# A fused attention and two-layer-pair MLP on one core: gathered score blocks in four fixed tiles, cleared once

## The chip, the core and the metric

The kernel runs on one core of a Trainium2 chip. The time is the device time of one execution in microseconds (us); before the change three runs gave a median of 1237.27 us. TensorE (PE) multiplies matrices, VectorE (DVE) and ScalarE (ACT) work elementwise and empty PE's accumulators, GpSimd (Pool) does small elementwise work, and SyncE (SP) issues every DMA. Each engine takes its instructions in the order in which the program lists them.

## What is computed

```python
scores = scale * np.matmul(q, k.transpose(0, 1, 3, 2))          # 4 batches, 12 heads, 448 rows, 64 wide
scores = np.einsum('bhij,hg->bgij', scores, w_pre)              # heads mixed
attn = softmax(scores)                                          # max, exp, sum + 1e-9, divide
attn = np.einsum('bhij,hg->bgij', attn, w_post)                 # heads mixed again
x = np.matmul(attn, v)                                          # -> (1792, 768)
h = x @ w_in;  y = (h * np.clip(h + 3, 0, 6) / 6) @ w_out       # 768 -> 2048 -> 768
out = (((y @ w1) * (y @ w2)) @ w3) @ w4                         # 768 -> 1024 -> 1024 -> 768
```

## The kernel before

The program is written by a planner. Every step (`plan.add`) has an engine or a choice of engines, a cost, a priority and the steps that it needs; `Plan.run` plays the steps through with these costs and writes each engine's instructions in the order that comes out. `URGE` is the table of offsets that sets the priorities, so a change of one number can move steps on every engine.

Attention runs in 92 blocks, 23 to a batch. A chunk of 100 to 120 query rows is scored (`sc`: PE, six steps per chunk, each emptied by ACT or DVE into a tile `s`). From batch 1 on, q and k are split first into a high and a low half by Pool (`qhl`, `khl`, a cast and a subtraction for each piece). Then each block goes through these steps:

1. `blank` (L461): Pool clears the upper 4 rows of a tile `g`, of which there are four. Rows 4 to 123 come from the next step; the clearing is needed since the matmuls read from row 0.
2. `gather` (L471): SP issues two DMAs that collect the 12 heads of ten query rows each out of `s` into `g`.
3. `premix` (PE, `pre`): four matmuls on `g` mix the heads.
4. `rowmax` (DVE, `m`), two `softexp` (ACT, `e`, with the sums in `z`).
5. `guard` (L496, Pool, or DVE when Pool is planned to be busy for longer than `pGuard`): adds 1e-9 to `z`; `recip` (DVE, `r`), `weigh` (DVE, `wt`).
6. `postmix` (PE, `post`): 32 small matmuls, emptied in two copies by ACT or DVE into `pth` or `ptl`.

After 11 or 12 blocks `values` (PE, `val`) multiplies by v. Scores, premix, postmix and values share four accumulator tiles `pp`. The MLPs follow (`up`, `dn`, `w`), and their first `up` steps are interleaved with the last blocks. They reuse the tiles of attention: `t`, `v` and `gs` lie in the tiles of `g` or `e`.

Of the kernel before, what the change touches and what calls it, by code (L numbers as in the profile page):

```python
# [11 lines left out]
F32 = mybir.dt.float32  # L12
F32R = mybir.dt.float32r
# [7 lines left out]
B, H, S, D = 4, 12, 448, 64  # L21
# [11 lines left out]
BEFORE = 64 - ROWS  # L33
# [16 lines left out]
def query_order():  # L50
# [9 lines left out]

URGE = dict(pPool=13.287, pACT=19737.186, pDVE=67509.792, pOut=0.285, pGuard=376.043, pCopy=1.57, pRest=75.72, pEvac=56.516, load0=33.466, load=-4.77, gather=-168.494, pre=-140.104, max=-8.516, exp=27.495, norm=15.87, post=2.04, evac=43.38, values=32.185, step=8.267, vload=-54.801, vload0=-30.207, lead=-15.369, begin=-9.6, consts=-75.04, moe=102.08, rows=-66.313, win=-123.444, wout=-22.784, w34=60.769, w2=92.263, unit0=3.845, unit1=6.661, down1=78.626, unit2=12.371, down2=55.186, wo=-0.083, wd=-56.448, narrow=-92.743, sums=98.663, w34us=69.836, pHalf=621.884, halve=10.141)


SHARED = dict(
    accs=("pth",), kraw=("q",), qraw=("q",), khl=("k",), qhl=("u",), act0=("s",), act3=("s",), t=("g", "e"), v=("g", "e"), gs=("g", "e"), graw=("k",),
    w=("k", "u", "w"), block=("w", "u", "k"), raw=("q", "raw", "e"), early=("w0", "w1", "w2", "k", "u"), first=("q", "r0", "r1", "r2", "raw"), stg=("x",), stage=("raw", "w"),
    wo=tuple(f"z{i}" for i in range(9)) + ("w0", "w1", "w2") + tuple(f"y{i}" for i in range(28)),
    wd=tuple(f"z{i}" for i in range(6, 9)) + ("w0", "w1", "w2") + tuple(f"v{i}" for i in range(28)),  # L70
# [160 lines left out]
def attention_moe(ctx: ExitStack, tc, qd, kd, vd, consts, w_in, w_out, w1, w2, w3t, w4, out):  # L231
    nc = tc.nc
# [25 lines left out]
    def pool(name, side=left, **kw):  # L258
# [11 lines left out]
    BUFS = {  # L270
        "s": (kp, [120, H, S], F32, 2), "k": (kp, [128, 2, S], F32, 6), "q": (kp, [128, 2, S], F32, 3), "u": (kp, [128, DM], F32, 4),
        "kraw": (kp, [128, 2, S], F32, 0), "qraw": (kp, [128, DM], F32, 0), "khl": (kp, [128, 2, S], F32R, 0), "qhl": (kp, [128, DM], F32R, 0),
        "e": (kp, [128, 2, S], F32, 4), "g": (kp, [128, 2, S], F32, 4), "gs": (kp, [128, 2, S], F32R, 0), "t": (kp, [128, 2, S], F32, 0),
        "act0": (kp, [128, 2, KC, S], F32R, 0), "act3": (kp, [128, 2, KC, S], F32R, 0), "o": (None, [128, 2, S], F32, 2),
        "v": (kp, [128, 2, S], F32, 0), "graw": (kp, [128, 2, S], F32, 0),
        "w": (None, [128, DM], F32R, 1), "raw": (None, [128, DM], I32, 3), "block": (None, [128, 2, DM // 2], F32R, 0),
# [21 lines left out]
    def take(*bufs):  # L298
        for x in bufs:
            shape, dtype = BUFS[x.kind][1:3]  # L300
            p, part, _, n = BUFS[x.tag]
            if p == "x":
                x.t = late["acts"][part // 4].rearrange("p a (h c) s -> p (a h) c s", h=2)[:, part % 4]
            elif p == "y":
                x.t = late["acts"][part // 7].rearrange("p a c s -> p (a c s)")[:, part % 7 * DM:(part % 7 + 1) * DM]
            elif p == "z":
                x.t = late["z"][part // 3][:, part % 3]
            elif p == "acts":
                x.t = late["acts"][part]
            elif isinstance(part, int):  # L310
                x.t = late[p][:, part]
            else:
                p = late[p or "pool"] if isinstance(p, (str, type(None))) else p
                x.t = p.tile(shape, dtype, tag=x.tag, name=x.kind, bufs=max(n, 1))
# [26 lines left out]
    direct, gathers, loads = [], {}, []  # L341
# [8 lines left out]
    def constants():  # L350
        raw = Buf("consts")
        dma_in(URGE["consts"], consts, raw, ns=300)

        def emit():
            x = raw.t
            own, own2 = x[:, 2 * H:2 * H + SET], x[:, 2 * H + SET:]
            nc.vector.memset(wih[:, ROWS:], 0.0)
            nc.vector.scalar_tensor_tensor(
                out=wih[:, :ROWS].rearrange("p (i g) -> p i g", i=SET), in0=x[:, :H].unsqueeze(1).to_broadcast([128, SET, H]),
                scalar=D ** -0.5, in1=own.unsqueeze(2).to_broadcast([128, SET, H]), op0=ALU.mult, op1=ALU.mult)  # L360
            nc.vector.tensor_tensor(
                out=wip, in0=x[:, H:2 * H].unsqueeze(2).to_broadcast([128, H, SET]),
                in1=own2.unsqueeze(1).to_broadcast([128, H, SET]), op=ALU.mult)
        plan.add("DVE", 700, -6, emit, use=(raw,))
# [88 lines left out]
    def mix(s):  # L453
# [4 lines left out]
        both = range(min(2, G0[4] - 2 * t))  # L458
        used = slice(0, PIECE * len(both))

        def blank():  # L461
            take(g)
            nc.gpsimd.memset(g.t[:BEFORE], 0.0)  # L463
        blanked = plan.add("Pool", 900, at + URGE["gather"] - 1, blank, new=(g,))
        for y in both:
            G = 2 * t + y
            c = next(c for c in range(4) if G < G0[c + 1])
            p0, d = G - G0[c], GROUPS[c]
            st = stile[4 * b + c]

            def gather(y=y, st=st, p0=p0, d=d):  # L471
                nc.sync.dma_start(out=g.t[BEFORE:BEFORE + 2 * ROWS, y], in_=st.t[p0:p0 + 9 * d + 1:d])  # L472
            gathers[s, y] = plan.add("SP", 1250, at + URGE["gather"], gather, read=(st,), after=(blanked,), hold=(g,), chain=("g", s), issue=760)
            g.writers.append(gathers[s, y])

        def premix():
# [68 lines left out]
    def values(prio, u, hq):  # L545
# [38 lines left out]
        for pr in range(2):  # L584
            stored.setdefault((u // 2, 2 * hq + pr), []).append(op)

    constants()
    for ci in range(16):
        s0 = cstart[ci - 1] * U0 + URGE["begin"] if ci else -120
# [573 lines left out]
```

## Time and profile before

| | us |
|---|---|
| three runs | 1231.84, 1237.27, 1242.02 |
| profiled execution, its own time | 1233.19 |
| its span, first to last instruction | 1231.4 |
| PE busy in it | 1201.4 |
| DVE, ACT, Pool busy in it | 798.5, 521.5, 220.2 |

The profiled execution took 1233.19 us by the clock of the runs, 1.8 us more than its span. A matmul counts as busy from its start to its modelled end, and matmuls overlap, so the idle time of PE is a surer figure than its busy time. "Issue" as a releaser stands for an idle time at whose end the profile sees no event.

### The profile page before, as it was taken

The numbers are of one execution on the slowest core, as the hardware profiler recorded it, in microseconds if no ns is written. First come the engines' busy times: TensorE is split into PE (matmuls) and PEld (weight loads), VectorE is DVE, ScalarE is ACT, GpSimd is POOL, SyncE is SP. The second block draws the span as 40 slices with busy tenths as digits, with TensorE's granted clock in tenths as the row PEclk, the third lists the DMA queues.
The fourth block names the chain that finished last, engine by engine and source line by source line (L and its number), as shares of the span: only waits on it lengthen the run. The fifth ranks groups of instructions, "written<-read, shape, count | busy, mean of one in ns | idle before, by whom it ended". The sixth has DMA issues, their size and how long they took to land.

```text
span 1231.4 us, 29262 instructions
## 1 busy us (share of the span) xinstructions
PE 1201.4 (98%) x12048; PEld 999.6 (81%) x12048; DVE 798.5 (65%) x1348; ACT 521.5 (42%) x1003; POOL 220.2 (18%) x428
## 2 busy tenths in 40 slices
PE   8899999999989999999999999999999999999998
PEld 3566656666668899999999999998889988999997
DVE  3787677767788789414777777417777688853210
ACT  7767566566664443212333333213433332332110
POOL 2476664844244200001000000000000000000000
PEclk9999999999999999999999999999999999999999
DMA  6654755736768777724899898716843222433311
GB/s 224 198 164 166 231 171 159 231 130 197 224 178 272 226 262 263 257 73 160 265 302 291 280 334 297 266 47 226 305 140 111 93 82 82 144 122 137 105 60 46
DMA packets 105357, 231.53 MB, mean 188 GB/s; under 512 B 10152, under 2 KB 53512, under 8 KB 105224
## 3 DMA queue, kind: packets, MB, share of 16 engines
q1 hardware_dynamic: 105224, 229.66, 56.6%
q8 instruction: 95, 1.56, 0.5%
q14 instruction: 38, 0.31, 0.1%
HBM read 132.31 MB, written 58.61 MB: 155 GB/s over the span
## 4 chain that ended last, share of the span: by engine, by line
PE 83%; DMA 4%; issue 3%; ACT 3%; POOL 2%; DVE 2%; SPq 2%; POOLq 0%; ACTq 0%; DVEq 0%
PE up L239 34%; PE dn L239 29%; PE w L239 5%; PE post L239 5%; PE sc L239 4%; PE pre L239 4%; PE val L239 3%; DMA qraw<-qd 1%; SPq L472 1%; DMA stg<-xdram 1%; ACT e L492 1%; POOL g L463 1%; ACT ptl L334 0%; DMA stage<-xdram 0%; ACT pth L334 0%
## 5 line engine op out<-in xcount | busy, mean ns | idle before, releaser
L239 PE MATMUL dn<-gs,act 128*128 128x448 f32 x1080 | 222.9, 366 | 0.0
L239 PEld LDWEIGHTS dn<-gs,act 128*128 128x128 f32 x1080 | 202.8, 188 | 17.5
L239 PE MATMUL up<-act,block 128*128 128x448 f32 x1008 | 206.8, 366 | 2.4 <-ACT t L1065 0.9
L239 PE MATMUL up<-act,w 128*128 128x448 f32 x1008 | 205.1, 365 | 0.0
L239 PEld LDWEIGHTS up<-act,block 128*128 128x128 f32 x1008 | 188.7, 188 | 20.1 <-ACT t L1065 2.1
L239 PEld LDWEIGHTS up<-act,w 128*128 128x128 f32 x1008 | 189.3, 188 | 14.5
L695 ACT ACTIVATE raw<-raw 128x384 f32<-128x384 f32 (+1 forms) x140 | 73.6, 528 | 172.4 <-DMA raw<-w 51.1
L239 PEld LDWEIGHTS post<-wt,e 60*64 60x64 f32 x5760 | 99.8, 135 | 55.3 <-issue 24.9
L492 ACT ACTIVATE e<-pre,m 128x448 f32<-128x448 f32 (+1 forms) x184 | 116.4, 635 | 35.6 <-DVE m L486 17.5
L486 DVE TENSOR_REDUCE m<-pre 128x2 f32<-128x896 f32 (+1 forms) x92 | 99.9, 1086 | 39.8 <-PE pre L239 39.5
L242 DVE TENSOR_TENSOR gs<-graw,gs 128x896 fp32r<-128x896 f32 x48 | 52.1, 1088 | 104.0 <-ACT gs L334 101.3
L239 PE MATMUL post<-wt,e 60*64 60x60 f32 x5760 | 107.1, 220 | 9.9 <-issue 4.2
L239 PE MATMUL dn<-gs,wo 128*128 128x448 f32 x456 | 101.6, 368 | 0.0
L463 POOL MEMSET g<- 4x896 f32 x92 | 76.6, 835 | 108.5 <-PE pre L239 95.2
L239 PE MATMUL pre<-g,wih 64*64 64x448 f32 x720 | 93.2, 560 | 2.6 <-issue 1.7
L239 PEld LDWEIGHTS dn<-gs,wo 128*128 128x128 f32 x456 | 85.6, 188 | 8.0
L242 POOL TENSOR_TENSOR early<-raw,wo 128x768 fp32r<-128x768 f32 x1 | 1.8, 1848 | 458.9 <-ACT wo L334 458.9
L334 ACT CAST gs<-graw 128x896 fp32r<-128x896 f32 x44 | 41.3, 939 | 91.4 <-PE dn L239 77.7
L710 DVE SCALAR_TENSOR_TENSOR raw<-raw 128x384 int32<-128x384 int32 (+1 forms) x140 | 71.7, 544 | 0.0
L708 DVE SCALAR_TENSOR_TENSOR raw<-raw 128x384 int32<-128x384 int32 (+1 forms) x140 | 70.6, 541 | 1.6
L817 DVE SCALAR_TENSOR_TENSOR t<-t,up 128x896 f32<-128x896 f32 x32 | 34.7, 1084 | 56.6 <-ACT t L814 56.1
L242 DVE TENSOR_TENSOR block<-raw,block 128x384 fp32r<-128x384 f32 x112 | 60.6, 560 | 14.7 <-ACT block L334 14.0
(87 smaller groups left out, 1496.7 us busy)
## 6 DMA issues: line engine op xcount, KB each, us to landing
g<-s SPq DMA_DIRECT2D x180, 210.0 KB
raw<-w SPq DMA_DIRECT2D x48, 384.0 KB
g1dram<-t SPq DMA_DIRECT2D x32, 448.0 KB
graw<-g1dram SPq DMA_DIRECT2D x32, 448.0 KB
raw<-w_out SPq DMA_DIRECT2D x32, 384.0 KB
raw<-w_in SPq DMA_DIRECT2D x28, 384.0 KB
raw<-w3t SPq DMA_DIRECT2D x32, 256.0 KB
g2dram<-t SPq DMA_DIRECT2D x32, 224.0 KB
```

The source lines that it names most:

```text
L239: nc.tensor.matmul(o, lhsT=lt, rhs=rh, start=start, stop=stop, **kw)
L242: eng.tensor_tensor(out=o, in0=a, in1=b, op=ALU.subtract)
L334: nc.scalar.copy(o, i)
L463: nc.gpsimd.memset(g.t[:BEFORE], 0.0)
L472: nc.sync.dma_start(out=g.t[BEFORE:BEFORE + 2 * ROWS, y], in_=st.t[p0:p0 + 9 * d + 1:d])
L486: nc.vector.tensor_reduce(out=m.t[used], in_=pre.t[used, :, :S], axis=AX.X, op=ALU.max, negate=True)
L492: nc.scalar.activation(out=e.t[used, a_], in_=pre.t[used, a_, :S], func=ACTF.Exp, bias=m.t[used, a_:a_ + 1], accum_out=z.t[used, a_:a_ + 1])
L695: nc.scalar.mul(value()[:, halves[i]], f(bits(i))[:, :, 1], 2.0 ** -112)
L708: two(out=y, in0=hi, scalar=-0x80000000, in1=y, op0=ALU.bitwise_and, op1=ALU.bitwise_or)
L710: two(out=y, in0=lo, scalar=29, in1=y, op0=ALU.logical_shift_right, op1=ALU.bitwise_or)
L817: nc.vector.scalar_tensor_tensor(out=t.t, in0=t.t, scalar=6.0, in1=p.t[:, :, :S], op0=ALU.min, op1=ALU.mult)
```

## The change

Four tiles `g0` to `g3` are allocated by name, one buffer each, and each is cleared once at the start by Pool. A block takes the lowest free one of them in the planner's play, and `take` hands it the fixed tile in place of a fresh one. The step of each block that cleared `g` becomes a step of the host, which writes no instruction. The kinds `t`, `v` and `gs` of the MLPs name the four tiles in place of `g`. Eighteen numbers of `URGE` differ too; those that bear on attention are `pGuard`, `load`, `norm`, `post`, `evac`, `values`, `step`, `vload`, `lead` and `halve`.

```diff
-URGE = dict(... pGuard=376.043, pCopy=1.57, ... load=-4.77, ... norm=15.87, post=2.04, evac=43.38, values=32.185, step=8.267, vload=-54.801, ... lead=-15.369, ... consts=-75.04, ... rows=-66.313, win=-123.444, ... down1=78.626, ... wo=-0.083, ... narrow=-92.743, ... w34us=69.836, ... halve=10.141)
+URGE = dict(... pGuard=295.919, pCopy=4.758, ... load=-12.417, ... norm=22.651, post=-48.647, evac=37.141, values=23.354, step=10.18, vload=-59.533, ... lead=6.488, ... consts=-27.952, ... rows=-164.737, win=-76.614, ... down1=80.329, ... wo=-28.358, ... narrow=-101.021, ... w34us=76.082, ... halve=-44.651)
+GS = tuple(f"g{i}" for i in range(4))
-    ... t=("g", "e"), v=("g", "e"), gs=("g", "e"), ...
+    ... g=GS, t=(*GS, "e"), v=(*GS, "e"), gs=(*GS, "e"), ...
-        "e": (kp, [128, 2, S], F32, 4), "g": (kp, [128, 2, S], F32, 4), ...
+        "e": (kp, [128, 2, S], F32, 4), **{t: (kp, [128, 2, S], F32, 1) for t in GS}, "g": (kp, [128, 2, S], F32, 0), ...
-            if p == "x":
+            if x.kind == "g":
+                x.t = late[x.tag]
+            elif p == "x":
-        def blank():
-            take(g)
-            nc.gpsimd.memset(g.t[:BEFORE], 0.0)
-        blanked = plan.add("Pool", 900, at + URGE["gather"] - 1, blank, new=(g,))
+        homed = plan.add("Host", 0, at + URGE["gather"] - 1, lambda: take(g), new=(g,), after=blanked)
-            gathers[s, y] = plan.add("SP", 1250, ..., after=(blanked,), hold=(g,), ...)
+            gathers[s, y] = plan.add("SP", 1250, ..., after=(homed,), hold=(g,), ...)
+    late.update({t: kp.tile([128, 2, S], F32, tag=t, name="g", bufs=1) for t in GS})
+    blanked = [plan.add("Pool", 850, -400, lambda t=t: nc.gpsimd.memset(late[t][:BEFORE], 0.0)) for t in GS]
```

Pool's instructions at the first halving of q and k (end of batch 0; `z` is a guard, `qhl` and `khl` are halves) stood like this before:

```order
L497 TENSOR_SCALAR z<-z 128x2
L463 MEMSET g 4x896
L378 CAST qhl<-qraw 128x120
L497 TENSOR_SCALAR z<-z 128x2
L242 TENSOR_TENSOR qhl<-qraw,qhl 128x120
L378 CAST qhl<-qraw 128x120 x2
L242 TENSOR_TENSOR qhl<-qraw,qhl 128x120 x2
L378 CAST qhl<-qraw 128x120 x2
L242 TENSOR_TENSOR qhl<-qraw,qhl 128x120
L463 MEMSET g 4x896
L242 TENSOR_TENSOR qhl<-qraw,qhl 128x120
```

On the same engine at the same place after the change:

```order
L497 TENSOR_SCALAR z<-z 128x2 x14
L381 CAST qhl<-qraw 128x120
L243 TENSOR_TENSOR qhl<-qraw,qhl 128x120
L381 CAST qhl<-qraw 128x120 x2
L243 TENSOR_TENSOR qhl<-qraw,qhl 128x120 x2
L381 CAST qhl<-qraw 128x120 x2
L243 TENSOR_TENSOR qhl<-qraw,qhl 128x120 x2
L381 CAST qhl<-qraw 128x120
L243 TENSOR_TENSOR qhl<-qraw,qhl 128x120
L381 CAST khl<-kraw 128x224
L243 TENSOR_TENSOR khl<-kraw,khl 128x224
```

The clearings are gone, and the halves of a chunk stand in one run with no guard among them. In all, Pool has 4 clearings of `g` after, 92 before, and 76 guards after, 83 before; the other guards are on DVE.

PE's instructions from the last block of batch 0 (the `pre` of two matmuls) to the first of batch 1, before:

```order
L239 MATMUL pre<-g,wih 64x448 x2
L239 MATMUL post<-wt,e 64x60 x32
L239 MATMUL sc<-khl,qhl 120x448 x24
L239 MATMUL post<-wt,e 64x60 x32
L239 MATMUL pre<-g,wih 64x448 x4
```

The same stretch of PE after the change:

```order
L240 MATMUL pre<-g,wih 64x448 x2
L240 MATMUL post<-wt,e 64x60 x32
L240 MATMUL sc<-khl,qhl 120x448 x6
L240 MATMUL val<-pth,vv 64x240 x8
L240 MATMUL post<-wt,e 64x60 x32
L240 MATMUL sc<-khl,qhl 120x448 x18
L240 MATMUL post<-wt,e 64x60 x32
L240 MATMUL sc<-khl,qhl 120x448 x18
L240 MATMUL post<-wt,e 64x60 x16
L240 MATMUL sc<-khl,qhl 120x448 x6
L240 MATMUL pre<-g,wih 64x448 x4
```

Six matmuls make one score step, so eight score steps stand between the two `pre` where four stood. From batch 1 on, runs of two or more score steps occur 17 times after the change and 6 times before. At the end of attention five lots of three `up` matmuls stand between the last `post` steps after the change, where before three lots of nine, six and six stood. From there on PE's order is the same but for small shifts.

## Rows read from the trace of the kernel before

**Rows 1.** The page: busy us of each engine (share of the span), instructions.

```profile
PE 1201.4 (98%) x12048; PEld 999.6 (81%) x12048; DVE 798.5 (65%) x1348; ACT 521.5 (42%) x1003; POOL 220.2 (18%) x428
```

**Rows 2.** Busy time by stretch: stretch, its length, each engine's busy us (instructions), granted clock.

```profile
0.00:5.20 5.20, 0.08 (x2) 0.11 (x2) 0.09 (x2) 1.28 (x1) 3.38 (x8) 1.00 0.67 197
...
20.00:333.00 313.00, 300.25 (x7136) 188.02 (x7133) 237.78 (x419) 209.38 (x496) 172.01 (x383) 1.00 0.60 188
333.00:365.35 32.35, 28.67 (x596) 20.75 (x594) 27.52 (x49) 19.34 (x45) 11.44 (x13) 1.00 0.64 194
365.35:412.00 46.65, 45.26 (x216) 39.98 (x216) 36.69 (x49) 21.49 (x38) 19.41 (x16) 1.00 0.80 257
412.00:1200.00 788.00, 785.52 (x3908) 719.63 (x3907) 494.77 (x829) 255.36 (x408) 12.92 (x7) 1.00 0.56 189
1200.00:1231.40 31.40, 26.84 (x132) 24.34 (x130) 0.00 (x0) 2.72 (x3) 0.00 (x0) 0.99 0.14 53
```

**Rows 3.** Waits of PE, 20 to 366 us: total us, times, longest us.

```profile
PE post L239 <- issue: 4.2, 3, 3.1
PE post L239 <- ACT e L492: 1.7, 1, 1.7
PE post L239 <- ACT ptl L334: 1.7, 7, 0.6
PE pre L239 <- issue: 1.7, 3, 0.8
PE post L239 <- ACT pth L334: 1.5, 9, 0.2
PE val L239 <- DVE act L242: 1.4, 1, 1.4
PE pre L239 <- POOL z L497: 0.9, 1, 0.9
...
PE sc L239 <- ACT pth L334: 0.9, 3, 0.4
```

**Rows 4.** Tile g: the clearings (min/median/max ns), and how long Pool stood before them (us, times).

```profile
L463 POOL MEMSET g<- x92: 834/834/838, 0.7 to 330.5; 4x896 f32 x92
...
  POOL g L463: 95.2, 63
```

**Rows 5.** Timeline at 218 us: start, us, engine, instruction [idle before it, releaser].

```profile
218.43 0.84 POOL L463 MEMSET g<- 4x896 f32 x1
...
219.35 0.21 POOL L497 TENSOR_SCALAR z<-z 128x2 f32<-128x2 f32 x1
...
219.59 0.17 DVE L503 RECIPROCAL r<-z 128x2 f32<-128x2 f32 x1 [2.45 <-POOL z L497]
...
220.36 0.98 PE L239 MATMUL pre<-g,wih 64*64 64x448 f32 x8 [0.95 <-POOL z L497]
```

**Rows 6.** Tile z: the guards on Pool and on DVE, min/median/max ns.

```profile
L497 POOL TENSOR_SCALAR z<-z x83: 206/213/593, 22.3 to 348.7; 128x2 f32<-128x2 f32 x79, 64x2 f32<-64x2 f32 x4
L497 DVE TENSOR_SCALAR z<-z x9: 151/503/1549, 60.2 to 232.0; 128x2 f32<-128x2 f32 x9
```

**Rows 7.** Timeline of Pool at 73 us, and of DVE there.

```profile
72.95 1.27 POOL L242 TENSOR_TENSOR khl<-kraw,khl 128x224 fp32r<-128x224 f32 x2
...
73.94 1.55 DVE L497 TENSOR_SCALAR z<-z 128x2 f32<-128x2 f32 x1
...
74.17 0.68 POOL L378 CAST khl<-kraw 128x224 fp32r<-128x224 f32 x2
74.81 0.65 POOL L242 TENSOR_TENSOR khl<-kraw,khl 128x224 fp32r<-128x224 f32 x1
```

**Rows 8.** Timeline of PE at 87 us and 237 us: runs of score steps.

```profile
86.99 1.47 PE L239 MATMUL sc<-khl,qhl 64*120 64x448 f32 x12
88.66 1.49 PE L239 MATMUL sc<-khl,qhl 64*120 64x448 f32 x12 [0.20 <-ACT ptl L334]
...
237.32 1.16 PE L239 MATMUL post<-wt,e 60*64 60x60 f32 x64 [0.57 <-DVE s L336]
```

More of the change, by code (lines that the diff above doesn't have):

```diff
@@ L59, in query_order @@
     return order
-URGE = dict(pPool=13.287, pACT=19737.186, pDVE=67509.792, pOut=0.285, pGuard=376.043, pCopy=1.57, pRest=75.72, pEvac=56.516, load0=33.466, load=-4.77, gather=-168.494, pre=-140.104, max=-8.516, exp=27.495, norm=15.87, post=2.04, evac=43.38, values=32.185, step=8.267, vload=-54.801, vload0=-30.207, lead=-15.369, begin=-9.6, consts=-75.04, moe=102.08, rows=-66.313, win=-123.444, wout=-22.784, w34=60.769, w2=92.263, unit0=3.845, unit1=6.661, down1=78.626, unit2=12.371, down2=55.186, wo=-0.083, wd=-56.448, narrow=-92.743, sums=98.663, w34us=69.836, pHalf=621.884, halve=10.141)
+URGE = dict(pPool=13.287, pACT=19737.186, pDVE=67509.792, pOut=0.285, pGuard=295.919, pCopy=4.758, pRest=75.72, pEvac=56.516, load0=33.466, load=-12.417, gather=-168.494, pre=-140.104, max=-8.516, exp=27.495, norm=22.651, post=-48.647, evac=37.141, values=23.354, step=10.18, vload=-59.533, vload0=-30.207, lead=6.488, begin=-9.6, consts=-27.952, moe=102.08, rows=-164.737, win=-76.614, wout=-22.784, w34=60.769, w2=92.263, unit0=3.845, unit1=6.661, down1=80.329, unit2=12.371, down2=55.186, wo=-28.358, wd=-56.448, narrow=-101.021, sums=98.663, w34us=76.082, pHalf=621.884, halve=-44.651)
+GS = tuple(f"g{i}" for i in range(4))
 SHARED = dict(
-    accs=("pth",), kraw=("q",), qraw=("q",), khl=("k",), qhl=("u",), act0=("s",), act3=("s",), t=("g", "e"), v=("g", "e"), gs=("g", "e"), graw=("k",),
+    accs=("pth",), kraw=("q",), qraw=("q",), khl=("k",), qhl=("u",), act0=("s",), act3=("s",), g=GS, t=(*GS, "e"), v=(*GS, "e"), gs=(*GS, "e"), graw=("k",),
     w=("k", "u", "w"), block=("w", "u", "k"), raw=("q", "raw", "e"), early=("w0", "w1", "w2", "k", "u"), first=("q", "r0", "r1", "r2", "raw"), stg=("x",), stage=("raw", "w"),
@@ L272, in attention_moe @@
         "kraw": (kp, [128, 2, S], F32, 0), "qraw": (kp, [128, DM], F32, 0), "khl": (kp, [128, 2, S], F32R, 0), "qhl": (kp, [128, DM], F32R, 0),
-        "e": (kp, [128, 2, S], F32, 4), "g": (kp, [128, 2, S], F32, 4), "gs": (kp, [128, 2, S], F32R, 0), "t": (kp, [128, 2, S], F32, 0),
+        "e": (kp, [128, 2, S], F32, 4), **{t: (kp, [128, 2, S], F32, 1) for t in GS}, "g": (kp, [128, 2, S], F32, 0), "gs": (kp, [128, 2, S], F32R, 0), "t": (kp, [128, 2, S], F32, 0),
         "act0": (kp, [128, 2, KC, S], F32R, 0), "act3": (kp, [128, 2, KC, S], F32R, 0), "o": (None, [128, 2, S], F32, 2),
@@ L472, in gather @@
                 nc.sync.dma_start(out=g.t[BEFORE:BEFORE + 2 * ROWS, y], in_=st.t[p0:p0 + 9 * d + 1:d])
-            gathers[s, y] = plan.add("SP", 1250, at + URGE["gather"], gather, read=(st,), after=(blanked,), hold=(g,), chain=("g", s), issue=760)
+            gathers[s, y] = plan.add("SP", 1250, at + URGE["gather"], gather, read=(st,), after=(homed,), hold=(g,), chain=("g", s), issue=760)
             g.writers.append(gathers[s, y])
```

## The prediction, written before the result was known

> **What bounds the kernel now.** I begin with the busy times. PE is busy for 98% of the span, DVE for 65%, ACT for 42%, Pool for 18% [rows 1]. A busy matmul may only be a waiting one, so the second view is the table by stretch, read for what PE lacks in each: 5.1 us in the first 5.2 us, when nothing has been loaded; 313.00 - 300.25 = 12.75 us in the steady part of attention; 32.35 - 28.67 = 3.68 us where attention goes over to the MLPs; 1.4 us just behind it; 2.5 us in all the MLPs to 1200 us; 4.6 us at the end, the last copies and stores [rows 2]. That is 30 us in all. Some 9.7 us of it, the start and the end, lies outside what the change touches. What any new order of steps can win is in the other 20.3 us, 1.6% of the time, and most of that in attention. The clock gives nothing: it stands at 1.00 of full speed, 2.4 GHz, in all stretches but the last, 0.99.
>
> The third view is what PE waits for between 20 and 366 us [rows 3]. The list has 13 rows, and none of them names a gather's DMA or a clearing of `g`. The blocks come in time: four tiles are enough. The waits are small ones: 5.9 us of "issue", 4.5 us for ACT to empty accumulators in 22 waits (the three rows of `pth` and `ptl` shown and two of 0.2 us), one of 1.7 us for an exponential, one of 1.4 us for a half of an activation, one of 0.9 us for a guard.
>
> **The clearings.** The change takes away 88 of 92 clearings, 88 x 0.835 = 73.5 us of Pool's time [rows 4]. Pool is not the bound, so that alone is worth nothing. What counts is that Pool stood still for 95.2 us before clearings, in 63 waits until PE had finished a `pre` [rows 4], and everything behind in Pool's queue stood too: guards and halves. Only where such a guard made PE wait does it show. That is one place: at 218.43 the clearing, at 219.35 the guard, then `recip` on DVE, which had been idle for 2.45 us, and PE idle for 0.95 us before its next `pre` [rows 5]. I credit that 0.95 us; bounds 0 and 0.95, since the list of rows 3 has no second wait for a guard. Four clearings remain, at the start, as before: nothing.
>
> **The gathers.** Each of them now waits for PE itself, where it waited for Pool, which had waited for PE. It starts at least 0.83 us earlier. Queued behind it on SP are loads of q, k, v and stores of x, and they move up too. PE did not wait for any of them after the start, so I cost the gain at nothing. If the lead of the gathers were used up, at two gathers for a block, the 0.83 us would come back as a gain, never as a loss.
>
> **Guards.** Guards that stood behind a clearing delayed DVE's `recip` and `weigh`, and so the copies behind these on DVE. Copies that come late are the 4.5 us of waits for emptied accumulators. I credit half of them, 2.2 us; bounds 0 and 4.5. Against this stand the seven guards that move from Pool to DVE. Before, nine ran on DVE, with a median of 503 ns and up to 1549 ns against 151 ns at best [rows 6]. The long one, at 73.94, lies wholly inside a chain of halves on Pool that leaves no gap [rows 7]. After the change such chains are longer. Seven more at the worst excess, 1.55 - 0.15 = 1.4 us, are 9.8 us of DVE. No wait of PE names a guard on DVE, so I take 0 on the path, and half of it, 4.9 us, as the bad end.
>
> The Trainium skill, in "SBUF — State Buffer", section "Who interferes with whom", says that DVE and GpSimd share a pair of ports under an exclusive lock, that a copy, cast or `tensor_scalar` on DVE can claim it, and that the one that comes second is blocked wholly. It also says that an instruction of GpSimd that only writes does not hinder a DVE instruction with two inputs. By that rule the guards on DVE are blocked by halves more than by clearings, and their excess stays or grows; the sum would be 7 x (0.503 - 0.213) = 2.0 us worse than mine if each of the seven took the median of the nine in place of Pool's 213 ns [rows 6] and all of it were exposed. That speaks against the change, and the 1549 ns agree with it.
>
> **The new order of PE.** Score steps stand in 17 runs of two or more, 11 more than before. A run takes accumulators faster than ACT and DVE empty them. The longest run of before, four steps, cost 0.20 us of waiting in its middle, and the run at 235 us cost 0.57 us in the `post` behind it [rows 8]. I take the lower price, since the run of four is the nearest to the new ones of three: 11 x 0.20 = +2.2 us; bounds 0 and 11 x 0.57 = 6.3 us. At the change of batch eight score steps without a `pre` let the softmax run dry, but then `val` steps of 1.6 to 1.8 us stand between the next three `pre`, which cover the time from a `pre` to its `post`; I cost it at nothing. Without that cover a dry start would cost one pass of max, two exponentials, guard and `weigh`, which no row here shows without overlap.
>
> **The handover.** The last `post` steps wait for an exponential (1.7 us) and `val` for a half of an activation (1.4 us) [rows 3], most of the stretch's 3.68 us [rows 2]. Now five lots of three `up` matmuls stand between these posts, so there is work to fill in, and Pool, which makes the other halves for `up`, has no clearings left in its way. But `up` in such small lots can wait itself for its next activation. I credit half, 1.8 us; bounds 0 and 3.7.
>
> **The sum.** -0.95 - 2.2 + 2.2 - 1.8 = -2.75 us, with ends at -0.95 - 4.5 - 3.7 = -9.2 us and +4.9 + 6.3 = +11.2 us. The profiled execution took 1233.19 us; it would be 1230.4. The median of the runs lies 4.1 us above that execution, so for a median I predict 1237.27 - 2.75, about 1234 us. The ends become 1228 and 1248.
>
> **Rivals.** First, a larger gain. The new order may fill nearly all of the gaps: if four fifths of the 20.3 us go, "issue" included, the time is 1237 - 16 = 1221 us. For it: these gaps are many small ones with different releasers, which a better interleaving can remove together. Against it: "issue" waits name no step of this program, and the MLP's 2.5 us are little touched.
>
> Second, slower. Pool now halves a whole chunk in one go. Six casts and six subtractions, and eight more instructions for k, keep it for several us; a guard that is due in that time either queues behind the run or goes to DVE and is blocked there for up to 1.55 us [rows 7]. There are 12 such chunks (three batches of four). If each holds up one block's `post` by 1.55 us and PE finds nothing else listed before it, 18.6 us are lost, and with the credits for evacuation gone the time is about 1237 - 2.75 + 18.6 = 1253 us. It decides from about 1.3 us at each chunk on (12.4 + 2.75, over 12). Against it: before, Pool was held up for 95.2 us at the clearings in exactly such stretches, and PE lost 0.9 us.
>
> Third, the change does not reach PE at all: clearings and late guards lay under PE's work, the new order exchanges one small wait for another, and the time stays at 1237 us. For it: no wait in rows 3 is for `g`.
>
> **How the numbers follow.** The runs of before span 1231.84 to 1242.02, 0.8%, so 1%, 12.4 us, is about what a measurement can tell from no change. My forecast has a chance of 0.57, the unchanged time 0.12, the larger gain 0.17, the loss 0.14. The first two lie within 1%: 0.69. Faster by over 1% (under 1224.9) 0.17, slower by over 1% (over 1249.6) 0.14. The range takes in the bounds of the sum and reaches for half of the larger gain, to 1222; above it ends with the bounds, at 1248.
>
> **What would show it.** Right: four clearings on Pool; PE's idle time from 20 to 333 us between 8 and 15 us; no wait of PE for a gather; waits of `post` behind runs of three score steps of 0.2 us; the handover with about 2 us idle. Wrong: rows of PE waiting for `z` or `wt` of more than 5 us in total, DVE guards near 1 us on average, or PE idle before `sc` for halves. I would be wrong above all if PE's own pace changes with the order, as when a step takes longer behind another kind of step; the sum counts idle time alone.

## The result, and the profile after

The changed kernel takes 1241.08 us (median of 22 runs, 1235.15 to 1250.18), the kernel before 1234.98 us in 22 runs beside it (1230.68 to 1242.02). The ratio is 1.0052, with a 95% interval of 1.0037 to 1.0068: by the ratio 6.4 us slower, where 2.75 us of gain were forecast. The runs also spread more: 15 us from the fastest to the slowest, against 11. Two runs of one experiment below, e4, fell in a slower state of the chip and are left out of its numbers.

The page of the changed kernel, busy us of each engine. Pool has lost 75 us [rows 1]; PE is busy 2.3 us longer:

```profile
PE 1203.7 (97%) x12048; PEld 1001.5 (81%) x12048; DVE 793.2 (64%) x1347; ACT 527.3 (43%) x1012; POOL 145.3 (12%) x332
```

Busy time by stretch after, to be read against [rows 2]. PE is idle for 14.15 us from 20 to 333 us (12.75 before) and for 5.26 us where attention goes over to the MLPs (3.68 before). New is the clock: 0.99 and 0.95, where it stood at 1.00:

```profile
20.00:333.00 313.00, 298.85 (x7096) 189.68 (x7096) 224.77 (x406) 210.52 (x496) 97.78 (x288) 0.99 0.61 183
333.00:365.35 32.35, 27.09 (x610) 19.17 (x604) 24.97 (x45) 19.75 (x47) 10.11 (x13) 0.95 0.64 189
...
412.00:1200.00 788.00, 784.66 (x3889) 715.85 (x3889) 500.11 (x837) 256.34 (x411) 17.83 (x10) 1.00 0.56 190
```

What PE waits for after, 20 to 372 us. Against [rows 3], the waits for accumulators (`pth`, `ptl`) are down from 4.5 to 1.8 us and the guard is gone. The waits for `s`, that is for a copy of scores behind a run of score steps, have grown to 4.1 us in seven (before, 0.6 us of `post` and 0.9 us of `val`), and new are 2.7 us put down to `r`:

```profile
PE post L240 <- issue: 6.6, 7, 2.8
PE post L240 <- DVE s L339: 2.9, 5, 0.6
PE post L240 <- DVE r L503: 2.7, 2, 2.6
PE post L240 <- ACT e L492: 2.2, 1, 2.2
PE sc L240 <- DVE s L339: 1.2, 2, 0.6
PE post L240 <- ACT ptl L337: 0.9, 1, 0.9
...
PE post L240 <- DVE ptl L339: 0.7, 1, 0.7
...
PE val L240 <- ACT ptl L337: 0.2, 1, 0.2
```

The clearings and the guards after (min/median/max ns), against [rows 4, 6]. There are four clearings, and the 16 guards on DVE are not slower but faster than the nine of before:

```profile
L588 POOL MEMSET g<- x4: 834/834/834, 0.7 to 3.1; 4x896 f32 x4
```

```profile
L497 POOL TENSOR_SCALAR z<-z x76: 206/213/579, 22.8 to 352.9; 128x2 f32<-128x2 f32 x72, 64x2 f32<-64x2 f32 x4
L497 DVE TENSOR_SCALAR z<-z x16: 158/259/696, 61.6 to 255.7; 128x2 f32<-128x2 f32 x16
```

Three gaps of PE stand out in its timeline after. The second is the plainest: a `post` is cut in two, 56 of its 64 matmuls run, nothing comes for 2.79 us, then the last 8. The first stands ahead of the eleventh `post`, in a stretch of `post` and `pre` without score steps. The third is at the handover:

```profile
51.07 0.95 PE L240 MATMUL pre<-g,wih 60*64 60x448 f32 x7
54.59 1.98 PE L240 MATMUL post<-wt,e 60*64 60x60 f32 x64 [2.57 <-DVE r L503]
56.31 1.53 PE L240 MATMUL pre<-g,wih 64*64 64x448 f32 x8
...
132.05 1.05 PE L240 MATMUL post<-wt,e 60*64 60x60 f32 x56
135.88 0.44 PE L240 MATMUL post<-wt,e 60*64 60x60 f32 x8 [2.79 <-issue]
136.25 3.72 PE L240 MATMUL sc<-khl,qhl 64*100 64x448 f32 x18
...
343.83 1.72 PE L240 MATMUL post<-wt,e 60*64 60x60 f32 x64 [2.19 <-ACT e L492]
```

The releaser of the first, `r`, is hardly its cause. Of the first eleven weighings, counted on DVE from the start, the eleventh is this one, and with its 0.27 us it was over at 51.13, 3.5 us ahead of that `post`:

```profile
50.86 0.27 DVE L508 TENSOR_TENSOR wt<-wip,r 128x120 f32<-128x120 f32 x1
```

The first two gaps have something else in common: a packet of the queue named "instruction" lands in them. This is that queue between 133.2 and 134.4 us (packets, MB, share of the engines' time); between 52.0 and 53.2 us it has one as well, and so has the kernel before in its gap of 3.1 us, between 55.2 and 56.4 us:

```profile
q8 instruction: 1, 0.02, 4.8%
```

The places of such stops are fixed. Counted in the trace, PE has 24,314 instructions (weight loads, matmuls and semaphore instructions) for the 95 packets of this queue, 256 for each. In the traces of the kernel before, of the changed one and of e5 to e9 below, PE stops in attention 36 times for 0.5 us or more with "issue" as the releaser. In 35 of the 36, the matmul with which it goes on is number 193 or 194 in its block of 256 instructions (counted from 0); behind the stop put down to `r` it is number 195. In 34 of the 35, PE goes on 1.2 to 1.6 us after a packet of this queue has landed.

What follows each of the three is slow: a `post` of 1.98 and 1.72 us where one takes 1.16, eighteen score matmuls in 3.72 us where the other such runs take 2.1. The granted clock is lower there (stretches of 4 us, columns as above):

```profile
52.00:56.00 4.00, 1.43 (x55) 1.44 (x56) 2.08 (x6) 1.34 (x4) 0.21 (x1) 0.76 0.67 166
56.00:60.00 4.00, 3.93 (x128) 2.64 (x125) 2.11 (x5) 2.71 (x7) 1.29 (x5) 0.81 0.78 227
...
136.00:140.00 4.00, 3.94 (x30) 2.40 (x34) 1.85 (x3) 2.39 (x5) 0.00 (x0) 0.57 0.57 156
...
344.00:348.00 4.00, 3.99 (x71) 2.49 (x67) 2.64 (x5) 2.95 (x7) 1.39 (x3) 0.57 0.06 18
```

A mean of 0.57 over 4 us is 3.4 us at the lower level, 1.2 GHz (4 x 0.43 / 0.5), which costs 1.7 us of PE's work; the first drop lies across two of the stretches, 4 x (0.24 + 0.19) / 0.5, the same 3.4 us. All three together are some 5 us, nearly the whole difference of the two profiled spans, 1237.2 against 1231.4 us. But that neat account is of one execution only, as the experiments show.

### The profile page after: what moved, and what is told of

Read it like the earlier page. It is cut to its first block, busy times and chain, and to the rows that moved or that the text cites. A ratio compares the mean times of both kernels' runs of the same rounds, so it can differ in the third digit from the quotient of the medians.

```text
span 1237.2 us, 29170 instructions
## 1 busy us (share of the span) xinstructions
PE 1203.7 (97%) x12048; PEld 1001.5 (81%) x12048; DVE 793.2 (64%) x1347; ACT 527.3 (43%) x1012; POOL 145.3 (12%) x332
## 3 DMA queue, kind: packets, MB, share of 16 engines
q8 instruction: 95, 1.56, 0.5%
## 4 chain that ended last, share of the span: by engine, by line
PE 64%; ACT 1%; DVE 0%; issue 0%; DMA 0%; ACTq 0%; DVEq 0%
PE up L240 31%; PE dn L240 29%; PE w L240 5%; ACT t L337 0%; DMA raw<-w3dram 0%; DVE of L243 0%; ACT act L337 0%; ACT w L337 0%; ACT t L1067 0%; ACT o L337 0%; DVE w L243 0%; DVE t L1074 0%; DVE block L243 0%; ACT v L1067 0%; DVE v L1070 0%
## 5 line engine op out<-in xcount | busy, mean ns | idle before, releaser
L240 PE MATMUL post<-wt,e 60*64 60x60 f32 x5760 | 109.8, 222 | 16.1 <-issue 6.6
L240 PE MATMUL pre<-g,wih 64*64 64x448 f32 (+1 forms) x720 | 95.2, 555 | 0.9 <-ACT e L492 0.5
L337 ACT CAST block<-raw 128x384 fp32r<-128x384 f32 x81 | 40.6, 514 | 68.3 <-PE up L240 34.3
L240 PE MATMUL w<-w 128*128 128x512 f32 (+1 forms) x384 | 67.6, 338 | 0.1
```

The source lines that it names most:

```text
L240: nc.tensor.matmul(o, lhsT=lt, rhs=rh, start=start, stop=stop, **kw)
L337: nc.scalar.copy(o, i)
```

## The experiments

**The tiles or the order.** The diff does two things: it changes the tiles and it changes 18 numbers, from which the planner makes another order. Four kernels took parts of it.

`e1_fixed_old_numbers` is the changed kernel with this line back:

```diff
-URGE = dict(... pGuard=295.919, pCopy=4.758, ... post=-48.647, ... rows=-164.737, win=-76.614, ... halve=-44.651)
+URGE = dict(... pGuard=376.043, pCopy=1.57, ... post=2.04, ... rows=-66.313, win=-123.444, ... halve=10.141)
```

> Four fixed tiles, cleared once, as in the changed kernel, but all 18 numbers of the order as before, so that steps alternate again (14 pairs post then pre without a score step between them, 47 in the changed kernel, 10 before). Theory A (the new order of PE's steps costs the 6 us, the tiles nothing): 1233 to 1237 us, ratio to before 0.998 to 1.002, no gap of PE over 2 us with half a clock behind it in attention except at the handover. Theory B (the fixed tiles and their gathers, which wait for PE themselves, cost it): 1240 to 1243 us, ratio 1.004 to 1.007. If the clearings alone were worth what the prediction credited (0.95 + half of 4.5 us): ratio 0.997 to 0.998.

Measured: 1255.89 us, ratio 1.0176 (1.0149 to 1.0202).

`e2_cleared_new_numbers` is the kernel before with that line from the changed kernel.

> A clearing for each block as before, but all 18 numbers of the order as in the changed kernel. The planner then makes an order between the two (30 pairs post then pre; 10 before, 47 changed). Theory A (order): slower than before, 1237 to 1242 us, ratio 1.002 to 1.006, with gaps of PE of over 2 us in stretches of post and pre without score steps, and the granted clock at 0.5 to 0.6 just behind them. Theory B (fixed tiles): 1233 to 1237, ratio 0.998 to 1.002. Theory D (clearings in a Pool queue that also holds long runs of halves hold up guards): slower than the changed kernel, ratio to before over 1.007, with waits of PE for wt or for DVE.

Measured: 1277.24 us, ratio 1.0357 (1.033 to 1.0385), with 14 issue waits of `post` in attention, 14.5 us in all, and 10.1 us of waits for `wt`.

`e3_fixed_old_attention` is the changed kernel with attention's twelve numbers of before (`pGuard` to `halve`), `e4_fixed_old_mlp` with the six of the MLPs (`rows`, `win`, `down1`, `wo`, `narrow`, `w34us`).

> The changed kernel with the twelve numbers that place attention's steps as before, and the six that place the MLPs' loads and steps as changed. Theory A1 (3.8 us of the loss lie in attention by its order, 1.8 us in the second MLP by the MLPs' numbers): 1236 to 1238 us, ratio to before 1.001 to 1.003, and the last up at some 1113 us of the span. Theory A2 (all of it follows attention's order, the MLPs' loss too, being an after-effect): ratio 0.998 to 1.002. Theory A3 (all of it from the MLPs' numbers): ratio 1.004 to 1.007.

> The changed kernel with the six numbers that place the MLPs' loads and steps as before, and attention's twelve as changed (48 pairs post then pre). Theory A1 (3.8 us in attention by its order, 1.8 us by the MLPs' numbers): 1238 to 1240 us, ratio to before 1.003 to 1.004, and the PE gap of 2.2 us at the handover shorter or gone, the gaps at 52 and 133 us still there. Theory A2 (attention's order alone): ratio 1.004 to 1.007. Theory A3 (MLPs' numbers alone): ratio 0.998 to 1.002.

Measured: 1284.02 us, ratio 1.0401 (1.0369 to 1.0434), and 1248.9 us, ratio 1.0111 (1.0074 to 1.0148). All four are slower than either parent. Only theory D had said so, for e2 alone, and the waits for `wt` that it named are there; but e2 has an order of its own as well, so they don't settle it. The likely reason lies in the method: for each mixture the planner makes a third order that nobody had tuned. In e1 PE then stands idle for 7.5 us just behind the handover, at a clock of 0.85 (before 1.4 us [rows 2]):

```profile
365.35:412.00 46.65, 39.18 (x239) 31.23 (x238) 33.40 (x59) 20.99 (x42) 11.56 (x11) 0.85 0.68 226
```

So these four say that numbers and tiles are tuned to each other, and nothing on which of them costs the 6 us. For that the order has to be held fixed.

**The tiles at a fixed order.** `e5_old_order_cleared_once` leaves the planner of before as it is, with its 900 ns for each clearing, and only leaves out the clearings after a tile's first; `g` gets the four fixed tiles:

```diff
         def blank():
             take(g)
-            nc.gpsimd.memset(g.t[:BEFORE], 0.0)
+            if g.tag not in cleared:
+                cleared.add(g.tag)
+                nc.gpsimd.memset(g.t[:BEFORE], 0.0)
```

> The kernel before with its own order of steps kept on PE, DVE, ACT and SP, instruction by instruction; only the clearings go: four fixed tiles, each cleared at its first block alone, 88 clearings fewer on Pool, each gather waiting for PE itself. The planner still reckons with a clearing for each block, so that nothing else moves. What the prediction credited for clearings and guards (0.95 + 2.2 us): 1231 to 1233 us against 1234, ratio 0.997 to 0.998. Theory A (the clearings lay under PE's work and all the loss comes with the new order): ratio 0.998 to 1.001. Theory B (the fixed tiles cost): ratio 1.003 or more.

`e6_new_order_cleared_each` is the changed kernel with the clearing put back where the tile is taken, unknown to the planner:

```diff
-        homed = plan.add("Host", 0, at + URGE["gather"] - 1, lambda: take(g), new=(g,), after=blanked)
+        def blank():
+            take(g)
+            nc.gpsimd.memset(g.t[:BEFORE], 0.0)
+        homed = plan.add("Host", 0, at + URGE["gather"] - 1, blank, new=(g,), after=blanked)
```

> The changed kernel with its own order of steps kept on PE, DVE, ACT and SP, instruction by instruction; a clearing of the block's tile is put back on Pool for each block, 92 in all. Theory A (the order alone costs): ratio to before 1.003 to 1.008, as the changed kernel. If the clearings are in the way of the longer runs of halves on Pool: 1.010 or more, with waits of PE for wt or DVE. If the clearings hide as before: no more than 1 us over the changed kernel.

`e7_fixed_again` is the changed kernel, unaltered.

> The changed kernel once more, for a second trace. Ratio to before 1.004 to 1.007. If the three long gaps of PE in attention (at 52, 133 and 342 us, each with half a clock for 3.4 us behind it) belong to the order, they stand at the same places again; if instructions that come late are a matter of chance, the two issue gaps stand elsewhere, and only the gap behind the exponential at 342 us stays. If the second half of the second MLP is slow by its placement, the up steps with a block take 213 us again, 211 before.

Measured: e5 1234.38 us, ratio 0.9988 (0.9967 to 1.001); e6 1247.55 us, ratio 1.012 (1.0087 to 1.0153); e7 1238.96 us, ratio 1.006 (1.0028 to 1.0093). The tiles alone cost nothing that can be told from noise: theory B falls. The loss comes with the order: 1.0052 - 0.9988 = 0.64% (some 0.26% either way), 7.9 us. That is the order of steps on all engines; no run moves PE's alone. And leaving out the clearings, worth about 1.5 us in the old order, is worth some 8 us in the new one (1.012 against 1.0052), which theory A had not expected. In e6 PE waits for `s` and `wt` more, and has more issue waits:

```profile
PE post L240 <- issue: 8.5, 10, 1.6
PE post L240 <- DVE s L339: 5.0, 5, 1.7
PE val L240 <- issue: 2.8, 2, 1.4
PE post L240 <- DVE wt L511: 1.9, 2, 1.5
```

The second trace of the changed kernel, e7, has a span of 1231.1 us, as short as that of before and 6.1 us shorter than the first. Two of the three gaps of the first are not there (at the place of the 2.57 us PE stands for 0.76 us); instead PE stops inside a `post` at 302 us, and a `post` that follows takes 1.98 us. Only the gap at the handover is in both, 2.19 us each time. The timeline of e7:

```profile
300.77 1.10 PE L240 MATMUL post<-wt,e 60*64 60x60 f32 x61
303.24 0.33 PE L240 MATMUL post<-wt,e 60*64 60x60 f32 x3 [1.37 <-issue]
...
305.54 1.36 PE L240 MATMUL sc<-khl,qhl 64*100 64x448 f32 x6 [0.59 <-DVE s L339]
306.83 1.98 PE L240 MATMUL post<-wt,e 60*64 60x60 f32 x64
```

So PE can stop at one place in each block of 256 instructions, as counted above; in which blocks it does, and for how long, changes from one execution to the next, and one execution is no measure of it. The mean granted clock, which each run lists, is one: it is 0.9959 over 29 runs of the changed kernel and 0.9984 over 29 of before. Against full speed that is 1241 x 0.0041 = 5.1 us lost, and 1235 x 0.0016 = 2.0 us before, so about 3 of the 6 us are lower clock; the rest must be idle time and stretched steps.

**Why instructions come late.** The page has a DMA queue of kind "instruction" with 95 packets, 1.56 MB. PE has 24,096 matmuls and weight loads, or 254 for each packet. Two pairs of kernels, each with the new and the old order and four fixed tiles, lighten this supply. In the first, most gathers are left out, which takes the DMA share in attention from 0.61 to 0.23:

```diff
+                if (g.tag, y) not in fed:
+                    fed.add((g.tag, y))
-                nc.sync.dma_start(out=g.t[BEFORE:BEFORE + 2 * ROWS, y], in_=st.t[p0:p0 + 9 * d + 1:d])
+                    nc.sync.dma_start(out=g.t[BEFORE:BEFORE + 2 * ROWS, y], in_=st.t[p0:p0 + 9 * d + 1:d])
```

> The changed kernel with its order kept; it leaves out every gather but the first into each half of the four tiles (8 of 180 transfers remain), so that blocks after the fourth work on old scores. Theory S1 (PE's instructions come late in dense stretches because they share the DMA engines with the gathers): issue waits of PE in attention under 1.5 us against 4.9 to 6.6, mean granted clock 0.998 or more against 0.996, 1233 to 1236 us, ratio to before 0.998 to 1.001. Theory S2 (they come late because post uses them up faster than they can come, whatever the other traffic): issue waits of 4 us or more and 1239 to 1243 us stay, ratio 1.003 to 1.007. Theory L (not instructions: the softmax of a block runs dry for want of score steps): post waits for e, r and wt of 3 us or more stay, clock drops behind them.

> The same with the old order and tiles cleared once: 8 of 180 gathers remain, blocks after the fourth work on old scores. Theory S1: issue waits under 1.5 us against 5.7, 1229 to 1233 us, ratio to before 0.996 to 0.999; the distance between the two orders shrinks from 7 us to under 3. S2 and L: no change from 1234 us beyond 2 us, the distance stays at 5 to 8 us.

In the second, `post` needs half of the instructions for the same columns:

```diff
                 for k, k0 in enumerate(KEY0):
+                    if k // 2 % 2:
+                        continue
...
-                        mm(post.t[o, y, c0:c0 + ROWS], e.t[i, a_, k0:k0 + PIECE], w.t[i, a_], True, True)
+                        mm(post.t[o, y, c0:c0 + 2 * ROWS], e.t[i, a_, k0:k0 + PIECE], w.t[i].rearrange("p a r -> p (a r)"), True, True)
```

> The changed kernel with its order kept; each post step works out its sums with half of the matmuls, each twice as wide (16 for 32 in the program, 120 columns for 60), so half of its sums are those of other keys. The columns on PE stay, the instructions halve. Theory S (either form; instructions come late in dense post and pre): no issue waits in post after 40 us, clock 0.998 or more, and the two orders stand within 2 us of each other. Theory L: post waits for e, r and wt stay at 3 us or more, or grow if post becomes shorter; clock 0.996, the distance between the orders stays at 5 us or grows. The absolute time says little: a post of 1.16 us may become shorter, by at most some 0.4 us x 92.

> The same with the old order and tiles cleared once: half of the post matmuls, twice as wide. Theory S: no issue waits in post after 40 us, and within 2 us of the new order with wide post. Theory L: 5 us or more faster than the new order with wide post, since score steps between post and pre give the softmax time.

Measured, new order and old: with few gathers 1228.69 us (0.9953, 0.9932 to 0.9974) and 1226.34 us (0.9937, 0.9914 to 0.996); with the wide `post` 1221.72 us (0.9906, 0.9879 to 0.9933) and 1223.57 us (0.9909, 0.9879 to 0.9939). The distance of the orders shrinks from 0.64% to 0.16% with few gathers and to nothing with the wide `post`, each with 0.3 to 0.4% either way.

The first pair does not bear out theory S1, although the distance shrank as it had said and both times are lower than it had said. Issue waits stay, in all 3.8 us in e8 and 5.1 us in e9, where S1 wanted less than 1.5. The row of `post` in e5, e8, e9:

```profile
PE post L240 <- issue: 4.6, 5, 1.5
```

```profile
PE post L240 <- issue: 2.6, 3, 1.0
PE post L240 <- issue: 4.1, 4, 1.7
```

The packets of the instruction queue took as long as ever, a median of 1.03 us in the changed kernel and 1.02 us in e8 and e9 (20 to 340 us). So it is not shown that the gathers make instructions late, and why both orders gain from fewer gathers is open.

In the second pair a `post` took 1.05 us for 1.16, 92 x 0.11 = 10.1 us in all; the old order gained 10.8 us over e5, about that, the new one 19.4 us over the changed kernel. The difference, 8.6 us (8.3 by the ratios, some 6 us either way), is what the new order gets back besides when `post` needs half of the instructions. Its trace has one issue wait left, of 0.3 us at the start, and the queue has lost 23 packets for 5,760 instructions, 250 each, so these packets are PE's instructions. The queue of the changed kernel, then of e10:

```profile
q8 instruction: 95, 1.56, 0.5%
```

```profile
q8 instruction: 72, 1.18, 0.4%
```

That all of the 8.6 us were late instructions is not shown: the edit halves the weight loads of `post` too, and the mean clock of e10 is 0.9974 (0.9987 in e11), where theory S wanted 0.998 or more.

Theory L, a softmax that runs dry, is not the main cause: its waits stay (2.1 us for `e` and 1.4 us for `wt` in e10), and the distance went all the same.

The stage from 20 us to the first `dn` matmul, one row for each kernel, shows what the new order asks of PE (of the changed kernel and e7 the row of the MLPs too). In the order before, changed, e7, e5:

```profile
20.00:582.00 562.00, 544.17 (x8784) 407.31 (x8781) 404.30 (x677) 303.71 (x654) 211.80 (x417) 1.00 0.62 199
```

```profile
20.00:585.80 565.80, 544.47 (x8788) 409.60 (x8785) 396.42 (x675) 309.82 (x665) 137.94 (x322) 0.99 0.63 198
585.80:1237.20 651.40, 644.33 (x3193) 585.18 (x3192) 395.23 (x669) 204.71 (x333) 4.01 (x3) 1.00 0.52 177
```

```profile
20.00:581.70 561.70, 541.76 (x8785) 408.42 (x8782) 397.49 (x675) 309.24 (x664) 138.30 (x322) 1.00 0.64 199
581.70:1231.10 649.40, 642.30 (x3193) 585.37 (x3191) 395.59 (x669) 205.15 (x333) 3.96 (x3) 1.00 0.52 178
```

```profile
20.00:579.50 559.50, 543.60 (x8784) 408.60 (x8781) 396.55 (x677) 303.48 (x654) 139.84 (x330) 1.00 0.62 200
```

And e8 and e9 (few gathers), e10 and e11 (wide `post`):

```profile
20.00:573.70 553.70, 536.59 (x8792) 405.99 (x8785) 399.70 (x675) 309.73 (x665) 137.42 (x322) 1.00 0.42 136
```

```profile
20.00:576.90 556.90, 543.57 (x8795) 407.98 (x8794) 396.96 (x678) 305.24 (x655) 141.52 (x330) 1.00 0.42 135
```

```profile
20.00:568.10 548.10, 531.80 (x5908) 393.24 (x5905) 396.67 (x675) 309.53 (x665) 138.27 (x322) 1.00 0.64 204
```

```profile
20.00:573.60 553.60, 537.72 (x5912) 391.31 (x5905) 396.59 (x678) 304.75 (x655) 139.60 (x330) 1.00 0.63 202
```

The old order keeps PE busy for 543.6 us with or without gathers. The new one needs 541.8 and 544.5 us with all gathers, 536.6 us with few, 7 us less than the old, and 5.9 us less with the wide `post`. PE has the same matmuls in both. Much of it is in the score steps: alone, one takes 0.85 to 0.87 us, and three side by side take 2.1 us. Busy time on the tile `sc` alone, 20 to 366 us, in e7 and e5:

```profile
20.00:366.00 346.00, 65.01 (x472) 37.34 (x468) 40.29 (x37) 40.47 (x45) 1.00 0.62 185
```

```profile
20.00:366.00 346.00, 69.77 (x472) 35.25 (x468) 41.43 (x38) 39.81 (x44) 1.00 0.61 189
```

It is 66.2 us after against 69.4 before, 65.3 in e8 against 70.2 in e9, and 64.9 in e10 against 70.7 in e11; part of that is overlap with the step beside. So runs of score steps are cheaper for PE, by 3 to 6 us in each pair. In the runs' times this doesn't show beyond noise: e8 is 2.4 us slower than e9, e10 1.9 us faster than e11. The traces flatter the new order here, since those of e8 and e10 lie below their medians (1226.72 and 1220.72 us) and those of e9 and e11 above (1228.13 and 1225.18 us). With all gathers and all instructions, gaps, stretched steps and the lower clock take it back and more.

The rows behind 581.7 and 585.8 us hold a part that I can't settle: the MLPs took 651.4 us in the first trace of the changed kernel and 649.4 in the second, with nothing changed. This 2 us came in e8 (651.2 us) and partly in e10 (650.8 us) as well, and in none of the traces of the old order.

**Half of the instructions, the same sums.** The last four take the keys in four pieces of 128 in place of eight of 64:

```diff
-KEY0 = [56 * c for c in range(7)] + [S - PIECE]
+KEY0 = [112 * c for c in range(3)] + [S - 2 * PIECE]
...
-                        mm(post.t[o, y, c0:c0 + ROWS], e.t[i, a_, k0:k0 + PIECE], w.t[i, a_], True, True)
+                        mm(post.t[:, y, c0:c0 + ROWS], e.t[i, a_, k0:k0 + 2 * PIECE], w.t[i, a_], True, True)
```

> The changed kernel with its order kept; each post step takes its keys in four pieces of 128 in place of eight of 64, so that it needs half of the matmuls and weight loads (16 for 32 in the program) for the same sums. Theory S (instructions come late): no issue wait in post beyond 0.3 us, mean granted clock 0.997 or more, ratio to before 0.988 to 0.993, within 2 us of the old order with paired post. Theory L (softmax runs dry): the distance to the old order with paired post stays at 4 us or more. If a post with 128 columns of weights takes as long as now (1.16 us) or longer, the ratio of both orders rises, but S still wants them equal.

> The old order, tiles cleared once, post in four pieces of 128 keys. Theory S: ratio to before 0.988 to 0.993, as the new order. Theory L: 4 us or more faster than the new order with paired post.

> The kernel before with a clearing for each block, post in four pieces of 128 keys. If the clearings hide under PE's work even when PE is not held up by instructions: within 2 us of the old order cleared once. If the shorter steps bring them out: 2 to 5 us slower than that.

> The new order with a clearing for each block, post in four pieces of 128 keys. Cleared once against cleared each was worth 6 to 8 us in the new order and 1 us in the old. If the clearings bite because the new order bunches the halves on Pool: 4 us or more slower than the new order cleared once with paired post. If they bit only through late instructions: within 2 us of it.

Measured, e12 to e15: 1307.42 us, ratio 1.0552 (1.052 to 1.0584); 1304.67, 1.0534 (1.0501 to 1.0568); 1301.38, 1.0516 (1.0484 to 1.0547); 1301.44, 1.0521 (1.0486 to 1.0555). A `post` now takes 2.0 us, as in this row of e12:

```profile
120.75 2.00 PE L240 MATMUL post<-wt,e 60*128 60x60 f32 x32
```

92 x 0.84 = 77 us more, of which 66 us show in e12 over the changed kernel and 70 us in e13 over e5. As a faster kernel this fails. As a test it says that with half of the instructions and longer steps the orders stand level (0.18% apart, intervals overlapping), and that clearing each block costs nothing in either of them (e14 and e15 are no slower than e13 and e12): e15, with 92 clearings in the new order, is 54 us over e6 only, so that the 8 us which they cost there are gone. Since longer steps also give the softmax more time, it separates the two theories less well than the wide `post` did. No version here that keeps all the sums beats the kernel before beyond its interval; the nearest is e5.

## Why the prediction was wrong

The forecast was 1234 us, and the time 1241.08 us lies inside its range, 1222 to 1248; but the sign is wrong. Step by step:

**The step that failed** is the new order of PE. It was costed by the runs of score steps alone, and the sum "counts idle time alone": the clock was taken to stay at 1.00, and the "issue" waits, 5.9 us [rows 3], which "name no step of this program", got no term. Nor had the order's other side, 37 more pairs of `post` and `pre` without a score step between them (47 for 10). At fixed tiles the order cost 7.9 us (1.0052 less 0.9988), where handover and score runs stood in the sum with 2.2 - 1.8 = +0.4 us. Four things are in it. The mean clock fell, about 3 us of PE's time. PE stood at the places where its instructions come in, 8.3 and 5.6 us in the two traces of the changed kernel against 4.7 us in those of before and of e5 (stops of 0.5 us or more that end just behind a landed packet); halve the instructions of `post`, and these stops and the distance of the orders are gone. The handover and the waits for scores grew, as told below. Against these stand score steps that are cheaper by 3 to 6 us. How the 7.9 us divide among them in a typical run is not shown. The last sentence of the prediction named PE's pace as what would make it most wrong. The pace of score steps did change, but for the better; the loss came as idle time and lower clock.

**Score runs** were right in kind. Waits for a copy of scores rose from 1.5 us in two (0.57 us [rows 8], and 0.9 us of a `val`) to 4.1 us in seven; each costs 0.6 us and not the 0.2 us that I took, so that 2.6 us stand for 2.2, inside the bounds.

**The handover** went the other way: 5.26 us idle and 5.80 in e7, against 3.68, where a gain of 1.8 was credited. The five small lots of `up` stand behind the `post` that waits 2.19 us for its exponential, not ahead of it, and fill nothing there.

**Clearings, gathers and guards** were credited with 0.95 + 2.2 us. e5 measures them alone, 1.5 us, with an interval from a loss of 1.2 to a gain of 4.1 us: not told from nothing. The 4.5 us are 21 waits, not the 22 that the prediction counts; the 0.9 us of `val` are not among them. The wait for a guard behind a clearing is gone as said, and waits for accumulators fell from 4.5 us to 3.6 us in e5, so half of them was too much; in the changed kernel, with the new order, they fell to 1.8 us. No gather made PE wait in the first trace, as said, and one did for 0.2 us in e7.

**Guards on DVE** cost nothing, as taken. By the Trainium skill ("SBUF — State Buffer", "Who interferes with whom") the prediction had the excess stay or grow when halves take the place of clearings. What the Trainium skill says there of an instruction that only writes is for a DVE instruction with two inputs; a guard has one, so that does not follow. The trace has 16 of them with a median of 259 ns and a longest of 696 ns, against 503 and 1549 ns, and no wait of PE names one. Why the excess shrank is not shown.

**The rivals.** The slower one (chance 0.14) had the sign, but not the mechanism: Pool's long runs of halves held nobody up, as long as the clearings stayed away. (Its 1253 us still hold the credit for evacuation that it calls gone; without it they are 1255.) The surprise is e6: the clearings lie under PE's work in the old order and bite in the new, so leaving them out pays only with the new order, and there only with the `post` of 1.16 us (e15). "A larger gain" had its reason half right: score steps side by side are cheaper for PE, but the gaps did not go.

## What to carry to other kernels

Before crediting a denser order of small matmuls, count the instructions that it asks for in each microsecond, and look in the profile for "issue" waits in the middle of a step: an idle engine that nothing releases may be waiting for its own instructions. Count them in the trace: stops that always stand at the same place in a block of instructions are of this kind, whatever releaser the profile names. Where a planner makes the order, a change and its tuned numbers can't be taken apart by mixing them; hold the emitted order fixed and vary one thing in it. One profiled execution of a kernel that loses time by chance can show all of the loss or none of it; the mean clock over many runs told more here than either trace.

## What the runs showed of the hardware

Instructions of PE come in packets of 256 (24,314 for 95) through a DMA queue of their own, and in stretches of `post` (64 matmuls and 64 weight loads in 1.16 us) PE stood for up to 3.1 us with nothing else to wait for, at the same place in a block of 256 each time and until 1.2 to 1.6 us after a packet had landed. Halving the instructions took these gaps away. The Trainium skill, "Runtime: NRT & Kernel Launch", section "Instruction fetch mechanics", says that the next block of 256 instructions is fetched while the current one runs, and that this is mostly hidden. The size agrees (256 by the count above). Hidden it is in the MLPs, which show no such wait from 412 to 1200 us; in attention it is not.

A gap's length alone doesn't tell whether the clock falls behind it. It fell to 1.2 GHz for 3.4 us with gaps of 2.57, 2.79 and 2.19 us in one trace (in the first of them half a us before the gap's end), in e5 behind one of 1.59 us, and in e7 behind 1.37 and 0.59 us in short order; it didn't behind the 3.10 us in the kernel before, nor behind the same 2.19 us at the handover in e7.

A matmul with 128 columns of weights over 60 rows, in place of two with 64, halves the count and yet takes `post` from 1.16 to 2.0 us. The Trainium skill, "TensorEngine Tiling (Array Packing)", section "Key Properties", says that the tiles of the array load weights and multiply independently, in parallel. By that alone 32 matmuls on two tiles of 64 by 128 would take no longer than 64 on four tiles of 64 by 64. Here they take longer, and one part of it stands in the rows: a weight load took 188 ns for 128 columns and 135 ns for 64 (medians, e12 and the changed kernel):

```profile
L240 PEld LDWEIGHTS post<-wt,e x2880: 182/188/335, 27.0 to 425.1; 60*128 60x128 f32 x192
```

```profile
L240 PEld LDWEIGHTS post<-wt,e x5760: 129/135/228, 27.4 to 357.1; 60*64 60x64 f32 x199
```

It was not tried why.
